# Raw weight loads from the seventh first-layer piece on are begun by ScalarE instead of SyncE

## Chip, core and metric

The kernel runs on one core of one Trainium2 chip. The metric is the device time of one execution in microseconds (us). Before the change its median over 3 runs is 1234.65 us (1234.53 to 1234.99). PE is TensorE, DVE VectorE, ACT ScalarE, POOL GpSimd, SP SyncE; SP does no arithmetic here, it begins transfers.

## What is computed

Attention over 8 batches and 12 heads (448 positions, head width 64) with RMS-normalised q and k, followed by a two-layer network with an ELU over all 3584 positions. The reference, cut to what matters:

```python
q_n, k_n = rmsnorm(q, g_q), rmsnorm(k, g_k)
scores = scale * q_n @ k_n.T
attn = exp(scores - max) / (sum + 1e-9)
x = (attn @ v).transpose(0, 2, 1, 3).reshape(B * S, H * D)   # 3584 x 768
h = x @ w_in                                                # w_in 768 x 2048
g = where(h > 0, h, exp(min(h, 0)) - 1)
out = g @ w_out                                             # w_out 2048 x 768
```

## The kernel before

The work is cut into 48 pairs of heads with 7 score tiles each, and 8 batches of the network. Every fp32 operand is split into a high and a low fp16 part, so that each product is three fp16 matmuls. The weights go through the same splitting once, at the start: `w_in` in 16 pieces of 128 x 768 (768 KB as read), `w_out` in 24 pieces of 128 x 512 (512 KB as read). For each piece `conv` builds a list of steps: `load` (a transfer from device memory into a raw buffer, L228 to L231), `s_act` on ACT (absolute value, L237, the first reader of the raw bits), `s_bits` on ACT (L240), `s_shift` on DVE (L245), `s_join` on DVE (L269, the last reader of the raw buffer), `s_sums` on PE (L142), `s_scale` on DVE, `s_high` on POOL, `s_low` on DVE (L290, L312). There are six raw buffers for `w_in` (two in `raws`, four in `whos`) and two for `w_out`, so a later load waits until the piece that had its buffer has passed `s_join`.

Order is written out by hand. The table `SCHED` gives each step a time in half slots; `run_tasks` emits the steps of a half slot, loads of whole slots first. Every engine then works through its own instructions in exactly that order. All transfers, 750 of them, are begun by SP: loads of q and k (`nat`, L330), of v (L172, L338), of the weights (L229), transposes in the transfer engines (`qkt` L420, `ptall` L613), two copies per pair that swap the halves of the transposed q (`q_swap`, L427), and the output (L711). PE needs the swapped copy for the second matmul of each score tile (L537).

The other ACT steps that matter here: `s_exp` (L558), the copy of normalised scores out of PSUM that frees the bank (`s_hi`, L592 or L598), `qk_square` (L353), `k_high` (L391), `q_high` (L401).

Of the kernel before, what the change touches and what calls it, by code (L numbers as in the profile page):

```python
# [33 lines left out]
def tile_attention_then_elu_mlp(ctx: ExitStack, tc: tile.TileContext, qk, v, v_scan, gg, w_in, w_out, out):  # L34
# [13 lines left out]
    nc = tc.nc  # L48
# [76 lines left out]
    def room(all, width, i):  # L125
        n = all.shape[1] // width
        return all[:, i % n * width : i % n * width + width]

    def small(name, w=1, dt=F32, bufs=2):
        return pool.tile([128, w], dt, tag=name, name=name, bufs=bufs)  # L130
# [3 lines left out]
    def upper(t):  # L134

        return t.bitcast(BF16).rearrange("p (n w) -> p n w", w=2)[:, :, 1]

    def column_sums(parts, bank):


        for i, a in enumerate(parts + [tiny]):
            nc.tensor.matmul(bank[:, S:], ones, a, start=i == 0, stop=i == len(parts))  # L142

    def largest(bank, e):
        nc.vector.tensor_reduce(out=e, in_=bank[:, S:], axis=AX.X, op=ALU.max)  # L145
        return e
# [3 lines left out]
    def ibits(dst, src, s1, op0, s2, op1):  # L150
        nc.vector.tensor_scalar(
            out=dst.bitcast(I32), in0=src.bitcast(I32), scalar1=s1, scalar2=s2, op0=op0, op1=op1
        )
# [53 lines left out]
    def on_pe(fn):  # L207

        late.add(fn)
        return fn  # L210
# [7 lines left out]
    def conv(src, i, width, acol, bank, parts):  # L218

        raw = raw_in[i % len(raw_in)] if width == WI_W else room(raws, 2 * width, i)
        raw, raw16 = (r.rearrange("p (n w) -> p n w", n=width) for r in (raw, raw.bitcast(U16)))

        t, w = room(wts, width, i), room(w32s, width, i if width == WI_W else i + 2)
        ws = None

        def load():  # L228
            nc.sync.dma_start(  # L229
                out=raw, in_=src[i].bitcast(U32).rearrange("p (n w) -> p n w", w=2)  # L230
            )  # L231

        def s_act():

            nc.scalar.activation(t, raw[:, :, 1].bitcast(F32), AF.Abs, scale=2.0**-112)  # L237

        def s_bits():
            nc.scalar.activation(  # L240
                raw16[:, :, 2], raw16[:, :, 1], AF.Copy, scale=0.875 * 2.0**-13, bias=0.49
            )

        def s_shift():
            nc.vector.tensor_scalar(  # L245
                out=t.bitcast(U32), in0=t.bitcast(U32), scalar1=3, scalar2=None,
                op0=ALU.logical_shift_left,
            )

        def s_sums():  # L250
            column_sums([upper(t[:, a : a + 64]) for a in range(0, width, 64)], bank)

        def s_scale():
            nonlocal ws
            e = largest(bank, acol)
            ws = small("ws", bufs=4)

            ibits(ws, e, POWER, ALU.bitwise_xor, POWER, ALU.bitwise_and)
            if width == WO_W and i % 12 == 11:
                d = i // 4 - 2  # L260
                for r in range(4):
                    rows = slice(32 * r, 32 * r + 32)
                    ibits(
                        a_out[rows, d : d + 3], most[rows, 4 * d + r : 4 * d + 12 : 4],
                        POWER, ALU.bitwise_and, 0, ALU.bitwise_or,
                    )

        def s_join():
            nc.vector.scalar_tensor_tensor(  # L269
                out=w.bitcast(U32), in0=raw[:, :, 1], scalar=0x80000007, in1=t.bitcast(U32),  # L270
                op0=ALU.bitwise_and, op1=ALU.bitwise_or,
            )

        steps = [load, s_act, s_bits, s_shift, s_join, on_pe(s_sums), s_scale]
        for fn in parts:
            step = lambda fn=fn: fn(w, ws)
            steps.append(on_pe(step) if fn in late else step)
        loads.add(load)
        return steps

# [857 lines left out]
```

## Time and profile before

| | us |
|---|---|
| median of 3 runs | 1234.65 |
| the profiled execution, its own time | 1238.01 |
| its span on the core | 1236.2 |
| PE busy in the span | 1185.0 |
| DVE busy | 863.4 |
| ACT busy | 808.2 |
| POOL busy | 499.1 |

The profiled execution is one run; 1.8 us of its time lie outside the span of the recorded instructions. A busy PE is a PE with a matmul in flight. The times of the rows below are counted from the start of the span.

### The profile page before, as it was taken

How to read it: one execution, taken by the hardware profiler on the slowest of the kernel's cores; microseconds unless marked ns; L12 is line 12 of the kernel's file. 1: busy time of each engine (PE TensorE's matmuls, PEld its weight loads, DVE VectorE, ACT ScalarE, POOL GpSimd, SP SyncE). 2: the span in 40 equal slices, each digit the busy share in tenths (PEclk: the TensorE clock that was granted, in tenths of full speed). 3: DMA queues.
4: the chain of work that ended last, by engine and by line, in shares of the span. 5: the costliest groups of instructions: out<-in, count | busy, mean ns of one | idle time of the engine just before them, and what ended most of it. 6: DMA issues, size and time to landing. Idle time of an engine off the chain costs nothing.

```text
span 1236.2 us, 21611 instructions
## 1 busy us (share of the span) xinstructions
PE 1185.0 (96%) x7180; PEld 736.4 (60%) x7180; DVE 863.4 (70%) x2042; ACT 808.2 (65%) x1705; POOL 499.1 (40%) x789
## 2 busy tenths in 40 slices
PE   3778899999999999999999999999999999999998
PEld 2556455765557655675557655675557655675576
DVE  7889999888885588666885588566785588542410
ACT  7889999867775477556675477556675477542310
POOL 4767554644444343444344343444344344320000
PEclk9889999999999999999999999999999999999999
DMA  8766889879667876687668867687568766551000
GB/s 302 224 155 189 190 185 188 164 175 193 134 137 165 177 137 135 138 195 153 128 131 162 184 139 131 137 199 150 130 131 165 181 137 134 109 108 31 1 16 30
DMA packets 403024, 181.29 MB, mean 147 GB/s; under 512 B 368352, under 2 KB 385376, under 8 KB 402912
## 3 DMA queue, kind: packets, MB, share of 16 engines
q1 hardware_dynamic: 402912, 179.91, 66.8%
q8 instruction: 57, 0.93, 0.3%
q14 instruction: 55, 0.45, 0.1%
HBM read 68.35 MB, written 11.01 MB: 64 GB/s over the span
## 4 chain that ended last, share of the span: by engine, by line
PE 82%; DVE 4%; issue 0%; ACT 0%; POOL 0%; ACTq 0%
PE m L741 23%; PE m L730 22%; PE s L741 12%; PE s L730 11%; PE s L537 9%; PE av L630 7%; DVE p L603 1%; DVE st L544 0%; DVE gall L687 0%; DVE w32s L269 0%; DVE e L674 0%; DVE wlos L312 0%; PE av L142 0%; DVE wts L245 0%; ACT s L558 0%
## 5 line engine op out<-in xcount | busy, mean ns | idle before, releaser
L544 DVE TENSOR_REDUCE st<-s 128x1 f32<-128x448 f32 x336 | 207.3, 620 | 168.4 <-PE s L537 166.8
L741 PE MATMUL m<-gall,whos 128*128 128x448 f16 x1024 | 282.0, 353 | 0.0
L562 POOL TENSOR_SCALAR st<-st 128x1 f32<-128x1 f32 x294 | 74.3, 253 | 482.2 <-ACT s L558 475.2
L741 PEld LDWEIGHTS <-whos 128*128 128x128 f16 x1536 | 221.7, 144 | 73.4 <-issue 0.7
L730 PE MATMUL m<-x,whi 128*128 128x448 f16 x926 | 256.4, 353 | 0.3 <-DVE e L674 0.3
L558 ACT ACTIVATE s<-s,st 128x448 f32<-128x448 f32 x294 | 178.1, 606 | 100.0 <-DVE st L544 98.6
L730 PEld LDWEIGHTS <-whi 128*128 128x128 f16 x1536 | 149.8, 98 | 137.2 <-issue 1.7
L598 ACT ACTIVATE p<-s,st 128x448 f16<-128x448 f32 x294 | 185.1, 631 | 61.2 <-DMA ptall<-p 35.9
L603 DVE SCALAR_TENSOR_TENSOR p<-s,st,p 128x448 f16<-128x448 f32 x294 | 198.6, 677 | 30.8 <-ACT p L598 29.6
L537 PE MATMUL s<-qkt 128*128 128x448 f16 (+1 forms) x768 | 184.8, 360 | 18.0 <-ACT gall L592 5.3
L741 PE MATMUL m<-gall,wlos 128*128 128x448 f16 x512 | 181.3, 354 | 0.0
L730 PE MATMUL m<-x,wli 128*128 128x448 f16 x463 | 163.3, 353 | 0.0
L741 PE MATMUL s<-gall,whos 128*128 128x448 f16 x512 | 140.8, 353 | 0.0
L741 PEld LDWEIGHTS <-wlos 128*128 128x128 f16 x768 | 110.6, 144 | 41.6 <-issue 6.8
L730 PE MATMUL s<-x,whi 128*128 128x448 f16 x450 | 124.0, 352 | 0.0
L730 PEld LDWEIGHTS <-wli 128*128 128x128 f16 x768 | 75.1, 98 | 74.2 <-issue 6.8
L537 PEld LDWEIGHTS <-qkt 128*128 128x128 f16 (+1 forms) x768 | 63.3, 101 | 79.4 <-issue 34.5
L684 ACT ACTIVATE gall<-e,ui 128x448 f16<-128x448 f32 x128 | 85.1, 665 | 32.1 <-DVE e L679 32.1
L630 PE MATMUL av<-ptall,vt 128*64 128x448 f16 x924 | 94.7, 353 | 0.6 <-DVE most L145 0.6
L687 DVE SCALAR_TENSOR_TENSOR gall<-e,ui,gall 128x448 f16<-128x448 f32 x128 | 88.0, 688 | 8.5 <-ACT gall L684 8.3
L382 POOL TENSOR_TENSOR nat<-nat,r 128x896 f32<-128x896 f32 (+1 forms) x48 | 84.4, 1758 | 21.8 <-DVE r L372 13.5
L741 PE MATMUL s<-gall,wlos 128*128 128x448 f16 x256 | 90.6, 354 | 0.0
(120 smaller groups left out, 1696.5 us busy)
## 6 DMA issues: line engine op xcount, KB each, us to landing
nat<-in_qk SPq DMA_DIRECT2D x48, 448.0 KB, 4.6
raws<-in_w_out SPq DMA_DIRECT2D x24, 512.0 KB, 4.1
qkt<-qkt SPq DMA_DIRECT2D x96, 112.0 KB, 4.1
out<-y SPq DMA_DIRECT2D x48, 224.0 KB, 2.4
vn<-in_v SPq DMA_DIRECT2D x38, 256.0 KB, 3.0
vscan<-in_v_scan SPq DMA_DIRECT2D x36, 224.0 KB, 3.2
whos<-in_w_in SPq DMA_DIRECT2D x10, 768.0 KB, 6.6
ptall<-p SPq DMA_TRANSPOSE x336, 3.0
```

Source lines behind the costliest of these rows:

```text
L382: nc.gpsimd.tensor_tensor(out=n[:, a:], in0=n[:, a:], in1=r[:, a:], op=ALU.mult)
L537: nc.tensor.matmul(ps[r0 : r0 + n, :S], lhs, qq[:, 1, h * S : h * S + S], start=(t == 0), stop=(t == 2),)
L544: nc.vector.tensor_reduce(out=st[:, 0:1], in_=pss[T][:, :S], axis=AX.X, op=ALU.max, negate=True)
L558: nc.scalar.activation(e, ps, AF.Exp, bias=st[:, 0:1], accum_out=st[:, 1:2])
L562: (nc.vector if by_pe(T) else nc.gpsimd).tensor_scalar(out=st[:, 1:2], in0=st[:, 1:2], scalar1=1e-9, scalar2=2.0 ** (UP - 7) if by_pe(T) e ...
L598: nc.scalar.activation(p16[:, :S], pss[T][:, :S], AF.Copy, scale=stats[T][:, 2:3])
L603: nc.vector.scalar_tensor_tensor(out=p16[:, S:], in0=ps[:, :S], scalar=r, in1=p16[:, :S], op0=ALU.mult, op1=ALU.subtract)
L630: nc.tensor.matmul(av[64 * h : 64 * h + 64, :S], vs[:, h], ps[h], start=(k == 0), stop=(k == len(terms) - 1),)
L684: nc.scalar.activation(g[:, 0], e, AF.Copy, scale=ui)
L687: nc.vector.scalar_tensor_tensor(out=g[:, 1], in0=e, scalar=ui, in1=g[:, 0], op0=ALU.mult, op1=ALU.subtract)
L730: nc.tensor.matmul(ph[:, :S], w[:, c, :], x[:, r, :], start=(c == 0 and i == 0), stop=last)
L741: nc.tensor.matmul(py[:, :S], w, g[:, r, :], start=(f == 0 and i == 0), stop=last)
```

## The change

The transfer of `load` is begun by SP for the first six pieces of `w_in`, and by ACT for the other ten and for all 24 pieces of `w_out`. Nothing else differs: same half slots, same buffers, same sizes.

```diff
         def load():
-            nc.sync.dma_start(
+            eng = nc.sync if src is w_in and i < 6 else nc.scalar
+            eng.dma_start(
                 out=raw, in_=src[i].bitcast(U32).rearrange("p (n w) -> p n w", w=2)
             )
```

The order on PE, DVE and POOL is the same in both kernels; 34 transfers leave SP's list and stand in ACT's. Code below line 228 is one line further down in the changed kernel, so L237 there is L238, L558 is L559, and so on. `whos<-in_w_in` and `raws<-in_w_in` are loads of `w_in`, `raws<-in_w_out` of `w_out`; `wts<-` is `s_act`, `raws<-raws` and `whos<-whos` are `s_bits`, `ex,st<-` is `s_exp`, `gall<-` and `ptall<-` with 112x4x128 are `s_hi`.

First place: ACT, where the load of the last `w_in` piece comes in. Before:

```order
L558 ACTIVATE ex,st<-s_69,st 128x448
L592 ACTIVATE gall<-s_67 112x4x128
L558 ACTIVATE ex,st<-s_70,st 128x448
L592 ACTIVATE gall<-s_68 112x4x128
L237 ACTIVATE wts<-whos 128x768
```

After:

```order
L559 ACTIVATE ex,st<-s_69,st 128x448
L230 DMA whos<-in_w_in 128x1536
L593 ACTIVATE gall<-s_67 112x4x128
L559 ACTIVATE ex,st<-s_70,st 128x448
L593 ACTIVATE gall<-s_68 112x4x128
L238 ACTIVATE wts<-whos 128x768
```

The load now stands three ACT instructions ahead of `s_act`, which reads what it brings.

Second place: ACT, a little later, at the second piece of `w_out`. Before:

```order
L558 ACTIVATE ex,st<-s_67,st 128x448
L240 ACTIVATE raws<-raws 128x512
L558 ACTIVATE ex,st<-s_68,st 128x448
L237 ACTIVATE wts<-raws 128x512
L558 ACTIVATE ex,st<-s_69,st 128x448
```

After:

```order
L559 ACTIVATE ex,st<-s_67,st 128x448
L241 ACTIVATE raws<-raws 128x512
L230 DMA raws<-in_w_out 128x1024
L559 ACTIVATE ex,st<-s_68,st 128x448
L238 ACTIVATE wts<-raws 128x512
L559 ACTIVATE ex,st<-s_69,st 128x448
```

Here one ACT instruction lies between the load and its reader.

Third place: SP, around the swap copies (`qkt<-qkt`) of the second pair of heads. Before:

```order
L420 DMA_TRANSPOSE qkt<-t_249 128x7x128
L229 DMA whos<-in_w_in 128x1536
L427 DMA qkt<-qkt 64x896 x2
L229 DMA raws<-in_w_in 128x1536
L420 DMA_TRANSPOSE qkt<-t_402 128x7x128 x2
L229 DMA whos<-in_w_in 128x1536
```

After:

```order
L421 DMA_TRANSPOSE qkt<-t_249 128x7x128
L428 DMA qkt<-qkt 64x896 x2
L421 DMA_TRANSPOSE qkt<-t_402 128x7x128 x2
L428 DMA qkt<-qkt 64x896 x2
L331 DMA nat<-in_qk 128x896
```

The weight load that stood directly ahead of the two swap copies is gone from SP's list, and so is the one behind them.

## Rows read from the trace of the kernel before

**Rows 1.** Busy time by stretch: start:end, length, each engine, granted clock, DMA share, GB/s.
```profile
core 0: us, PE busy (x) PEld busy (x) DVE busy (x) ACT busy (x) POOL busy (x), PEclk, DMA share, GB/s
...
100.00:150.00 50.00, 41.50 (x348) 27.29 (x347) 47.42 (x141) 48.83 (x99) 32.02 (x40) 1.00 0.66 162
150.00:200.00 50.00, 47.12 (x330) 25.82 (x329) 48.75 (x115) 48.61 (x96) 25.38 (x37) 1.00 0.94 197
...
300.00:1100.00 800.00, 800.00 (x4647) 486.05 (x4647) 565.52 (x1323) 518.28 (x1156) 321.56 (x549) 1.00 0.72 148
```

**Rows 2.** Line 229 from 22 to 245 us: loads, ns min/median/max; time to landing.
```profile
L229 SPq DMA_DIRECT2D raws<-in_w_out x24: 327/336/1157, 87.9 to 239.3; - x24
...
DMA to landing us min/median/max: 3.4/4.5/9.0
```

**Rows 3.** The page's DMA issues: count, KB of one, median us to landing.
```profile
raws<-in_w_out SPq DMA_DIRECT2D x24, 512.0 KB, 4.1
qkt<-qkt SPq DMA_DIRECT2D x96, 112.0 KB, 4.1
```

**Rows 4.** SP's queue from 27 us: start, length, line, what it begins.
```profile
31.20 0.57 SPq L229 DMA_DIRECT2D whos<-in_w_in  x1
32.28 1.11 SPq L427 DMA_DIRECT2D qkt<-qkt  x2
```

**Rows 5.** Those two swap copies: who waited for them, and their time to landing.
```profile
  PE s L537: 1.7, 1
...
DMA to landing us min/median/max: 6.7/6.7/6.8
```

**Rows 6.** PE from 36 us: start, length, line, tiles, idle time before and releaser.
```profile
39.60 0.53 PE L537 MATMUL s<-qkt 128*128 128x448 f16 x1 [1.74 <-DMA qkt<-qkt]
```

**Rows 7.** Busy time by stretch, around that wait (columns of rows 1).
```profile
38.00:42.00 4.00, 2.40 (x13) 2.21 (x14) 2.88 (x11) 1.82 (x6) 2.62 (x5) 0.57 0.63 155
42.00:46.00 4.00, 4.00 (x30) 3.26 (x30) 2.61 (x9) 3.83 (x6) 2.42 (x3) 0.57 0.00 0
```

**Rows 8.** ACT from 43 us (columns of rows 6).
```profile
43.27 0.57 ACT L401 ACTIVATE t<-nat 128x448 f16<-128x448 f32 x1
...
47.80 0.94 ACT L237 ACTIVATE wts<-raws 128x768 f32<-128x768 f32 x1
```

**Rows 9.** ACT from 99 to 111 us (columns of rows 6).
```profile
100.26 0.62 ACT L558 ACTIVATE ex<-s,st 128x448 f32<-128x448 f32 x1
...
102.44 0.91 ACT L237 ACTIVATE wts<-whos 128x768 f32<-128x768 f32 x1
...
103.86 0.60 ACT L592 ACTIVATE gall<-s 112x512 f32<-112x512 f32 x1
...
108.35 1.34 ACT L240 ACTIVATE raws<-raws 128x512 uint16<-128x512 uint16 x1
...
110.21 0.67 ACT L237 ACTIVATE wts<-raws 128x512 f32<-128x512 f32 x1
```

**Rows 10.** PE from 102 us (columns of rows 6).
```profile
105.39 0.57 PE L537 MATMUL s<-qkt 128*64 128x448 f16 x4
```

**Rows 11.** ACT from 127 and from 150 us (columns of rows 6).
```profile
127.44 0.63 ACT L558 ACTIVATE ex<-s,st 128x448 f32<-128x448 f32 x1
...
130.76 0.66 ACT L237 ACTIVATE wts<-raws 128x512 f32<-128x512 f32 x1
...
150.80 0.66 ACT L666 ACTIVATE e<-e,one 128x448 f32<-128x448 f32 x1
...
154.26 0.68 ACT L237 ACTIVATE wts<-raws 128x512 f32<-128x512 f32 x1
```

**Rows 12.** ACT's queue at line 391 (ns, first and last start); ACT then.
```profile
L391 ACTq EVENT_SEMAPHORE  x1: 38/38/38, 94.9 to 94.9; - x1
...
94.19 1.94 ACT L240 ACTIVATE whos<-whos 128x768 uint16<-128x768 uint16 x1
```

**Rows 13.** SP's waits: waiting line, releaser: us in total, times, longest.
```profile
SPq L229 <- DVE w32s L269: 26.3, 11, 5.5
```

## The prediction, made before the result was known

> **What bounds the kernel now.** I first read busy time by stretch [rows 1]. From 300 to 1100 us PE is busy for all 800 us, at a granted clock of 1.00: there the kernel is bound by matmuls, their number is unchanged, and nothing that happens on ACT or SP can show in the time unless PE is made to wait. So the change is decided in the start-up, while weights are still being split. There PE is not full: 41.50 of 50 us from 100 to 150, 47.12 from 150 to 200. The engines beside it are: ACT has 48.83 and 48.61 of 50 us, DVE 47.42 and 48.75. All 34 moved loads lie between 22 and 240 us, 29 of them before 200. In that stretch ACT and DVE together set when PE gets its tiles, and ACT has 1.17 and 1.39 us of idle time in the two stretches of 50. Whatever is put on ACT there can hardly be absorbed. What PE loses before about 205 us is lost for good, since it is full afterwards.
>
> The second thing I read is who waits for transfers. PE's matmul at 39.60 us stood 1.74 us idle for a swap copy of q [rows 6]. The two swap copies were begun at 32.28 us, right behind a 768 KB weight load begun at 31.20 on the same queue [rows 4], and took 6.7 us to land [rows 5], where the median of all 96 is 4.1 [rows 3].
>
> **The change part by part.** *Taken from SP:* 34 issues, the 24 of `w_out` with a median of 336 ns [rows 2]; at that price they are 11.4 us of SP's own time, and the waits of these loads for their buffers. SP computes nothing; the one place where I see PE pay for it is the wait above, so I count only that.
>
> *Swap copies out of the load's shadow (term A).* With the load of 31.20 us gone to ACT, where its place comes some 6 us later, the swap copies can land nearer to the median, 2.6 us sooner (6.7 - 4.1). PE gains at most its wait, 1.7 us; I take -1.7. The far end: at 38 to 46 us the granted clock is 0.57 as a mean [rows 7], that is mostly the lower of the two levels, 1.2 GHz, and the fall came while PE was idle in this very wait. If the shorter wait kept PE at 2.4 GHz, the 2.40 and 4.00 us of busy time would shrink by the factor 0.57, by 1.0 and 1.7 us. The ends of A are 0 and -4.4.
>
> Here a rule of the Trainium skill speaks against the change. The row shows a copy that waited behind a load in one queue. "DMA: Bandwidth & Descriptors", section "Issuing engines are not separate DMA queues", says that transfers run on the same 16 DMA engines whoever begins them, and that a second issuer saves only the time to issue. By that rule A is 0, since the same bytes are moved, and the sum would be 1.7 us more; the row differs only in that the load also comes later.
>
> *Two loads that come too late (terms B and C).* In SP's queue a load ran well ahead of ACT. In ACT's list it can't be begun before ACT's own sequence reaches it, and its first reader, `s_act`, stands a fixed number of ACT instructions behind. If the transfer takes longer than these, ACT itself stops, and everything behind it on ACT: exponentials (DVE and POOL wait for their sums) and the copies that free PSUM banks for PE. The transfer takes 3.4 us at the least, 4.5 at the median of these loads, 9.0 at the most [rows 2].
>
> B: the last `w_in` piece stands behind the exponential that starts at 100.26 us, its reader started at 102.44 [rows 9], a gap of 2.2 us. With 4.5 us to land, ACT stops for 2.3 us. Ends: 1.2 (3.4 us to land) and 6.8 (9.0).
>
> C: the second piece of `w_out` stands behind the `s_bits` that starts at 108.35 us, its reader started at 110.21 [rows 9], a gap of 1.9 us. With the 4.1 us of loads of `w_out` [rows 3], ACT stops for 2.2 us. Ends: 1.5 (3.4) and 7.1 (9.0).
>
> B and C add up, since ACT works from 99 to 111 us without a pause: 4.5 us. What of it reaches PE: the copy of 103.86 us ends at 104.46, and PE's score matmul that needs its bank starts at 105.39 [rows 9, 10], so 0.9 us of B are slack there. Of ACT's own idle time, 1.17 us in this stretch, I let half absorb: 4.5 - 0.6 = 3.9 us are left on ACT's chain, and I count 3.9 as the delay of the end.
>
> *Further tight pairs (term D).* Five more pairs before 200 us have gaps like these two: 3.3 us (127.44 to 130.76) and 3.5 us (150.80 to 154.26) [rows 11]. At 4.1 us to land they would stop ACT by 0.8 and 0.6, the five together by about 3.7. Against it: ACT's queue runs ahead of its arithmetic. While `s_bits` ran from 94.19 to 96.13 us, the queue had already handled, at 94.9, the wait that belongs to the second instruction behind it (L391; L353 stands between) [rows 12]. So a load may begin up to two instructions earlier than I have put it, which at some 0.6 us each closes gaps of 0.8 and 0.6. I take 1.2, a third of 3.7; the ends are 0 and 3.7. The same running ahead would shorten B and C, whose shortfalls are too large to vanish. The loads of the pieces before have gaps of 4.5 us (43.27 to 47.80) [rows 8] and more, and I count them at nothing at a landing of 4.5; if a busy queue makes it 9.0, ACT stops for up to 4.5 there, partly in idle time.
>
> *Issue on ACT (term E).* Each issue takes ACT's queue about 336 ns, 29 of them before 200 us, 9.7 us in all [rows 2]. I take 0: most stand behind an instruction of 0.6 to 1.9 us, and the queue does its work under cover of that [rows 12]. If the cover is missing, the cost is 9.7 us, in a stretch without slack.
>
> *Waits added to ACT.* A load that waits for its buffer (for `s_join` on DVE) now holds ACT's list: behind it stand the exponentials and PSUM copies for which DVE and PE wait. SP stood 26.3 us in 11 such waits, 5.5 at the longest [rows 13], but it came early; ACT comes to the same place later, when DVE has mostly passed. I take 0; the far end is one full wait, 5.5 us. Below nothing it can't go, since ACT had no such wait.
>
> Sum: -1.7 + 3.9 + 1.2 + 0 + 0 = **+3.4 us**. Against the profiled execution of 1238.01 us that is 1241.4; that run is 3.4 us above the median of 1234.65, so against the median the forecast is 1234.65 + 3.4 = **1238.0 us**.
>
> **The rivals.**
>
> *Issue isn't covered (slower still).* Then E is 9.7 us at its end; 29 issues at 336 ns on an engine that is 97% busy. For: ACT's idle time is 2.56 us in 100 us [rows 1]. Against: the queue that runs ahead [rows 12]. Time: 1238.0 + 9.7 = 1247.7.
>
> *Nothing to be seen.* The running ahead closes D and most of B and C (two instructions of 0.6 us each, 1.2 off each of 2.3 and 2.2, leaves 2.1 on ACT), and A gives 1.7 back: +0.4, 1235.0. With no ACT stop and no gain at the swap copy, only SP's 11.4 us are saved, PE waits as before, and the time is 1234.7. That last is what the rule of the Trainium skill above comes to. That the change doesn't do what it says belongs here, and the order speaks against it: the loads do stand in ACT's list.
>
> *Faster.* The mechanism is the swap copy at 39.60 us and the clock behind it. If the copy lands over 1.7 us sooner and PE's clock then does not fall, A is -4.4. Together with the 2.1 of the case above, less the 0.9 of slack at 105 us [rows 9, 10], the sum is -4.4 + 2.1 - 0.9 = -3.2: 1231.4. It decides as soon as B and C together leave less than about 2 us. For: clock and wait stand in the rows. Against: ACT and DVE are so full behind it that a gain at 46 us has to pass through ACT's list, with a load in it at 43.27 us.
>
> **How the numbers follow.** Forecast (+1 to +6.5 us, by B, C and D at their nearer ends) 0.44; issue not covered 0.12; nothing to be seen 0.25; faster 0.19. The predicted time is that of the likeliest, 1238.0 us. The measurement can tell about 0.2%, 2.5 us. Of the forecast some 0.05 lie within that, and of the faster case 0.03: faster 0.16, same 0.33, slower 0.51. The range reaches into the faster case and, by half of E, into the uncovered one: 1231.5 to 1245.5 us, with about 0.1 left out on either side.
>
> **What would show it.** In the changed kernel's trace, `s_act` of the last `w_in` piece and of the second `w_out` piece should have idle time on ACT before them, ended by the transfers, of about 2 us each; PE should wait less for the swap copy near 39 us; PE's busy time should be full from a few us later than before. If ACT's idle time stands before instructions right behind an issue, E is the cause. If ACT waits nowhere for weights, B and C are wrong; if the low clock at 38 to 45 us is gone, the faster case is under way. A changed time with the same PE idle time before 205 us would overthrow the whole reading.

## The result, and the profile after

The changed kernel takes 1248.54 us in the median of 4 runs (1245.67 to 1256.08), the kernel before 1234.78 us beside it: a ratio of 1.0114, 95% interval 1.0089 to 1.0139, 13.8 us slower. The direction was forecast; the time lies 3 us above the range and 10.5 us above the predicted 1238.0.

The profiled execution took 1249.42 us. By stretch, with the columns of [rows 1]:

```profile
50.00:100.00 50.00, 38.13 (x311) 26.61 (x310) 39.96 (x103) 42.89 (x78) 31.52 (x34) 0.90 0.77 197
100.00:150.00 50.00, 41.34 (x335) 29.60 (x335) 42.92 (x127) 44.93 (x93) 28.46 (x37) 0.93 0.56 159
150.00:200.00 50.00, 45.22 (x300) 23.81 (x297) 46.93 (x111) 46.60 (x91) 25.66 (x37) 1.00 0.87 177
200.00:250.00 50.00, 46.95 (x319) 29.10 (x319) 42.52 (x99) 43.08 (x87) 23.95 (x35) 1.00 0.78 158
...
300.00:1100.00 800.00, 800.00 (x4654) 484.02 (x4652) 569.52 (x1328) 520.80 (x1162) 327.25 (x553) 1.00 0.73 150
```

As the prediction had it, nothing happens from 300 us on. Between 100 and 200 us ACT is no longer full: 8.5 us idle where it had 2.6 [rows 1]. PE's 41.34 us from 100 to 150 hide a loss, since part of that work ran at a lower granted clock (0.93). What the prediction did not expect stands in the line of 200 to 250 us. The same line of before:

```profile
200.00:250.00 50.00, 49.67 (x338) 31.64 (x336) 45.67 (x99) 43.24 (x83) 30.25 (x41) 1.00 0.80 170
```

PE was nearly full there, and now loses another 2.7 us.

The loads themselves, from 22 to 245 us, and what waited for them [rows 2]; then the page's DMA issues [rows 3]:

```profile
L230 ACTq DMA_DIRECT2D raws<-in_w_out x23: 334/335/637, 87.1 to 236.5; - x23
...
  ACT wts L238: 10.3, 7
...
DMA to landing us min/median/max: 3.4/4.5/9.8
raws<-in_w_out ACTq DMA_DIRECT2D x24, 512.0 KB, 4.0
```

An issue costs what it cost SP (335 ns against 336), and the median landing has not moved. But now `s_act` on ACT waits for loads, which was 1.0 us in before. The readers that wait, on ACT (start, length, line, tiles, idle time before and what ended it; the first is the last piece of `w_in`, the others pieces 1, 6, 10, 13, 18 and 22 of `w_out`, counted from 0):

```profile
105.89 0.91 ACT L238 ACTIVATE wts<-whos 128x768 f32<-128x768 f32 x1 [1.81 <-DMA whos<-in_w_in]
114.91 0.66 ACT L238 ACTIVATE wts<-raws 128x512 f32<-128x512 f32 x1 [1.46 <-DMA raws<-in_w_out]
136.36 0.68 ACT L238 ACTIVATE wts<-raws 128x512 f32<-128x512 f32 x1 [0.94 <-DMA raws<-in_w_out]
160.67 0.68 ACT L238 ACTIVATE wts<-raws 128x512 f32<-128x512 f32 x1 [0.20 <-DMA raws<-in_w_out]
177.15 0.68 ACT L238 ACTIVATE wts<-raws 128x512 f32<-128x512 f32 x1 [0.83 <-DMA raws<-in_w_out]
...
210.20 0.70 ACT L238 ACTIVATE wts<-raws 128x512 f32<-128x512 f32 x1 [2.05 <-DMA raws<-in_w_out]
...
241.91 0.68 ACT L238 ACTIVATE wts<-raws 128x512 f32<-128x512 f32 x1 [3.06 <-DMA raws<-in_w_out]
```

The first four have partners in [rows 9, 11]: they started at 102.44, 110.21, 130.76 and 154.26. So the delay against before grows from 3.5 to 4.7, 5.6 and 6.4 us, by 1.2, 0.9 and 0.8 us. The first two steps are about the idle time of the reader (1.46 and 0.94), the third is more than it (0.20). But 3.5 us are there already at the first, of which its own wait is only 1.8. The rest comes from an earlier place, on PE. In the kernel before PE had two waits near 75 us, after:

```profile
74.35 0.35 PE L537 MATMUL s<-qkt 128*128 128x448 f16 x1 [1.34 <-DMA qkt<-t]
76.82 1.28 PE L537 MATMUL s<-qkt 128*128 128x448 f16 x3 [2.12 <-DMA qkt<-qkt]
```

The same two in the changed kernel:

```profile
77.31 0.53 PE L538 MATMUL s<-qkt 128*128 128x448 f16 x1 [5.06 <-DMA qkt<-t]
78.33 1.28 PE L538 MATMUL s<-qkt 128*128 128x448 f16 x3 [0.49 <-DMA qkt<-qkt]
```

There PE waited 5.06 us for a transpose of the normalised q and k (`qkt<-t`), not for the swap copies. It leaves this place 1.5 us later than before (78.33 against 76.82). SP's queue, ACT's queue, and the time to landing of these two transposes:

```profile
64.38 3.55 SPq L421 DMA_TRANSPOSE qkt<-t  x2
64.80 0.36 ACTq L230 DMA_DIRECT2D raws<-in_w_in  x1
DMA to landing us min/median/max: 10.6/10.8/10.9
```

Ahead of all this lies what the change gains, the place of [rows 6, 7]:

```profile
38.80 0.54 PE L538 MATMUL s<-qkt 128*128 128x448 f16 x2 [1.43 <-ACT ptall L593]
42.00:46.00 4.00, 3.46 (x36) 2.62 (x36) 3.79 (x13) 4.00 (x9) 2.48 (x3) 1.00 0.86 261
```

The wait for the swap copy is gone (a wait of 1.43 us for ACT stands close to its place), and here the granted clock from 42 to 46 us is 1.00, not 0.57.

So the profile gives three candidates: loads that land after their reader is due ("late"), transposes that are slow beside loads of another queue ("beside"), and the issues on ACT ("issue", the rival of the prediction).

### The profile page after: what moved, and what is told of

Read it like the earlier page. It is cut to its first block, busy times and chain, and to the rows that moved or that the text cites. A ratio compares the mean times of both kernels' runs of the same rounds, so it can differ in the third digit from the quotient of the medians.

```text
span 1247.6 us, 21596 instructions
## 1 busy us (share of the span) xinstructions
PE 1190.4 (95%) x7180; PEld 739.8 (59%) x7180; DVE 864.5 (69%) x2042; ACT 808.2 (65%) x1705; POOL 496.5 (40%) x789
## 4 chain that ended last, share of the span: by engine, by line
PE 77%; DVE 2%; ACT 1%; issue 0%; DMA 0%; POOL 0%; SPq 0%; ACTq 0%; POOLq 0%
PE m L742 21%; PE m L731 21%; PE s L742 11%; PE s L731 10%; PE s L538 8%; PE av L631 6%; DVE wlos L313 0%; DVE p L604 0%; ACT p L599 0%; DVE st L545 0%; DMA ptall<-p 0%; DVE w32s L270 0%; ACT s L559 0%; DVE a_out L151 0%; DVE ss L358 0%
## 5 line engine op out<-in xcount | busy, mean ns | idle before, releaser
L559 ACT ACTIVATE s<-s,st 128x448 f32<-128x448 f32 x294 | 178.2, 606 | 99.5 <-DVE st L545 98.3
L383 POOL TENSOR_TENSOR nat<-nat,r 128x896 f32<-128x896 f32 (+1 forms) x48 | 84.5, 1760 | 21.3 <-DVE r L373 12.9
```

The costliest lines, as they stand in the source:

```text
L383: nc.gpsimd.tensor_tensor(out=n[:, a:], in0=n[:, a:], in1=r[:, a:], op=ALU.mult)
L559: nc.scalar.activation(e, ps, AF.Exp, bias=st[:, 0:1], accum_out=st[:, 1:2])
```

## The experiments

All ratios are against the kernel before on the same chip, with a 95% interval; its medians there were 1235.4 to 1235.9 us, so 0.001 is 1.2 us. Gains and losses in us are worked out from the ratio, which is not the quotient of the two medians: for e6 and e7 the medians lie 9.1 and 4.6 us apart, where the ratios give 7.8 and 3.7. Pieces are counted from 0.

**e1: 34 issues on ACT and nothing else.** The kernel before, with an additional transfer of 8 bytes per partition, begun by ACT, at each place of a moved load. Nobody reads what they bring.

```diff
+            if src is w_out or i >= 6:
+                k = 10 + i if src is w_out else i - 6
+                nc.scalar.dma_start(out=tinies[:, 2 * k : 2 * k + 2], in_=src[i].bitcast(U32)[:, :2])
```

> The kernel before, in which SP still begins all 34 weight loads; at the same places ACT begins 34 further transfers of 8 bytes per partition into a tile that nobody reads. So ACT pays for 34 issues and for nothing else. Theory 'late' (ACT stands still because the data of a late load isn't there) and theory 'beside' (a load on a second queue and a transpose on SP's queue slow each other) expect the time of the kernel before, within 1 us. Theory 'issue' (each issue stops ACT) expects 34 issues of 0.34 us, of which 29 lie where ACT is full: 5 to 10 us above before.

1235.22 us, ratio 0.9996 (0.9986 to 1.0007). Issuing on ACT costs nothing that can be measured; the rival "issue isn't covered" falls.

**e2 and e3: take one suspect out.** A list of the pieces whose load ACT begins takes the place of the change's condition, here and in most of what follows. e2 puts the seven loads that were waited for back on SP, e3 those beside slow transposes.

```diff
-            nc.sync.dma_start(
+            on_act = [6, 7, 8, 9, 10, 11, 12, 13, 14] if src is w_in else [0, 2, 3, 4, 5, 7, 8, 9, 11, 12, 14, 15, 16, 17, 19, 20, 21, 23]
+            (nc.scalar if i in on_act else nc.sync).dma_start(
```

> The changed kernel, with the seven loads for which ACT visibly stood still (w_in piece 15; w_out pieces 1, 6, 10, 13, 18, 22) given back to SP; 27 loads stay with ACT. The idle times of ACT before their first readers add up to about 10 us in the changed kernel's trace. 'Late' expects most of that back: 1248.5 - 7 to 10, that is 1239 to 1242 us. 'Beside' expects the loss between 55 and 78 us (about 4 us) to stay and the later ones to shrink only a little: 1245 to 1248. 'Issue' expects 7 of 34 parts of the loss back: about 1246.

1237.04 us, ratio 1.0026 (1.0005 to 1.0046).

```diff
+            on_act = [7, 8, 9, 10, 11, 13, 15] if src is w_in else [0, 1, 2, 3, 4, 5, 6, 7, 8, 9, 10, 11, 12, 13, 15, 16, 18, 19, 20, 21, 22, 23]
```

> The changed kernel, with five other loads given back to SP: those that took 7 us or more to land, or were in flight while SP's transposes took 7 us or more (w_in pieces 6, 12, 14; w_out pieces 14, 17). ACT does not stand still for any of them. 'Beside' expects the loss between 55 and 78 us (4 us) and that around 200 us (about 2 us) back: 1241 to 1244 us, and no transpose above 7 us there. 'Late' expects nothing back from it: 1247 to 1250. 'Issue' expects 5 of 34 parts back: about 1246.5.

1246.74 us, ratio 1.0087 (1.0068 to 1.0105). Most of the loss hangs on the seven late loads. What e3 gives back is less than its profile shows early on: its transposes near 64 us land after 3.3 and 4.6 us, and PE's matmul behind the swap copies starts 5.1 us earlier than in the changed kernel (73.22 against 78.33). But then ACT waits longer for pieces 1, 13 and 22 than in the changed kernel, and the reader of piece 22 starts only 3.1 us earlier:

```profile
73.22 0.91 PE L538 MATMUL s<-qkt 128*128 128x448 f16 x3 [1.72 <-DMA qkt<-qkt]
...
111.55 0.66 ACT L238 ACTIVATE wts<-raws 128x512 f32<-128x512 f32 x1 [2.34 <-DMA raws<-in_w_out]
...
174.36 0.67 ACT L238 ACTIVATE wts<-raws 128x512 f32<-128x512 f32 x1 [2.32 <-DMA raws<-in_w_out]
...
238.83 0.68 ACT L238 ACTIVATE wts<-raws 128x512 f32<-128x512 f32 x1 [3.73 <-DMA raws<-in_w_out]
```

So the losses by slow transposes and by late loads do not simply add. Back to e2: three of e2's ten runs lay at 1243.7 to 1244.2, the other seven at 1235.0 to 1237.8; more on that below.

**e4: the loads earlier in ACT's list.** If they are late, let them start sooner: each load up to 6 half slots earlier, as far as its buffer is free in the written order.

```diff
-        [56.5, 58.5, 60, 60, 62.5, 63, 67, 68.5, 70],
+        [50.5, 58.5, 60, 60, 62.5, 63, 67, 68.5, 70],
...
-        [51.5, 68.5, 70, 70.5, 71, 73, 77, 77, 78.5],
+        [47.0, 68.5, 70, 70.5, 71, 73, 77, 77, 78.5],
```

> The changed kernel, ACT begins the same 34 loads, but each up to 6 half slots earlier in ACT's list, as far as the raw buffer is free in the written order (w_in 15 and w_out 1 by 6 half slots; w_out 13, 18 and 22 by 0.5 to 1 only). 'Late' expects the idle times before the readers of w_in 15 and w_out 1 (3.4 us together) and part of those of w_out 6 and 10 to go: 1243 to 1246 us. 'Beside' expects no gain of that kind, since as many loads lie beside transposes: 1246 to 1252. 'Issue' expects no change: 1248.

1252.16 us, ratio 1.0135 (1.0116 to 1.0154): slower still. ACT's waits in it, from 20 to 245 us (us in total, times, longest):

```profile
ACT s L559 <- DVE w32s L270: 2.6, 2, 1.3
...
ACT wts L238 <- DVE w32s L270: 2.3, 1, 2.3
...
ACT wts L238 <- DMA raws<-in_w_out: 1.4, 2, 1.0
```

The waits for landings of weight loads have nearly gone, as "late" wanted. In their place ACT's instructions stand behind loads that wait for a buffer: L270 is `s_join` on DVE, the last reader of the raw buffer, which no exponential needs. ACT's waits for `s_join` come to 7.0 us in all, of a loss of 16.7; the rest was not divided further. In ACT's in-order list a load was too late for its reader or too early for its buffer. SP's list stood 26.3 us in such waits [rows 13], with no arithmetic behind them.

**e6 and e7: one suspect alone.** The seven late loads on ACT and all others on SP; then only the two of terms B and C.

```diff
+            on_act = [15] if src is w_in else [1, 6, 10, 13, 18, 22]
```

> The complement of e2: only the seven loads whose reader was seen to wait (the last w_in piece, w_out pieces 1, 6, 10, 13, 18, 22) are begun by ACT, all others by SP. 'Late' (a load in ACT's list lands after its reader is due, and ACT stops): these seven carry most of the loss, 1243 to 1246 against some 1235.4 for the kernel before, with ACT's s_act idle for transfers by 1 to 3 us each. 'Beside' (loads on a second queue hold up the transposes of t): with seven loads, none of them beside the transposes of 64 us, 1235 to 1238. 'Additive no' (a third reading: what is lost in one place is absorbed or made up by the others): between, 1238 to 1243.

1244.74 us, ratio 1.0063 (1.0044 to 1.0083): 7.8 us.

```diff
+            on_act = [15] if src is w_in else [1]
```

> Only the last w_in piece and the second w_out piece are begun by ACT: the prediction's terms B and C alone. The prediction's working gives +3.9 us for them, 1238 to 1241 with its ends wider. 'Late' by the trace of the changed kernel (idle time of 1.81 and 1.55 before the two s_act): +3.0 to +3.5, 1238 to 1239. 'Absorbed' (ACT's or PE's slack behind them takes it up): within 1 us of the kernel before, 1235 to 1236.5.

1240.24 us, ratio 1.0030 (1.0017 to 1.0043): 3.7 us. The two readers in e7:

```profile
102.90 0.92 ACT L238 ACTIVATE wts<-whos 128x768 f32<-128x768 f32 x1 [1.85 <-DMA whos<-in_w_in]
111.83 0.66 ACT L238 ACTIVATE wts<-raws 128x512 f32<-128x512 f32 x1 [1.37 <-DMA raws<-in_w_out]
```

3.2 us of idle time on ACT, 3.7 at the end: what ACT waits between 100 and 112 us is not absorbed. "Late" is shown as the largest part, by taking it out (e2) and by doing it alone (e6).

**e5, e9 and e10: the gain.** Five early loads on ACT; the one load of 31.20 us alone on ACT; and that load left on SP, but behind the two swap copies. In e10 nothing is on a second queue.

```diff
+            on_act = [7, 8, 9, 10, 13] if src is w_in else []
```

> Only w_in pieces 7, 8, 9, 10 and 13 are begun by ACT, loads that nobody was seen to wait for, and among them the one that the prediction's term A moves out of the swap copies' way (31.20 us). 'Late': nothing is lost, and if the 1.7 us of term A is real, 1233 to 1235; if it isn't, 1235 to 1236. 'Beside': any load on a second queue costs the transposes beside it something, 1236 to 1238.

1235.09 us, ratio 0.9987 (0.9975 to 0.9998).

```diff
+            on_act = [8] if src is w_in else []
```

> One load alone moves to ACT: w_in piece 8 (counted from 0), begun at 31.20 us before, directly ahead of the two swap copies. The prediction's term A alone: -1.7 us, with ends 0 and -4.4, so 1231 to 1235.5, most likely some 1233.9 against 1235.6 for the kernel before. If the swap copy's wait was nobody's loss: 1235 to 1236.

1234.92 us, ratio 0.9990 (0.9981 to 1.0000).

```diff
-        [11, 24, 27.5, 26.5, 28.5, 32, 31.5, 31.5, 38],
+        [11.5, 24, 27.5, 26.5, 28.5, 32, 31.5, 31.5, 38],
```

> The same load stays on SP, but stands behind the two swap copies instead of ahead of them (its half slot is 11.5 instead of 11). Nothing is on a second queue. 'The load merely stood ahead' (what the rule of the Trainium skill comes to: who begins a transfer does not matter, only when): the same gain as with the load on ACT, 1.7 us, some 1233.9, and PE no longer waits for the swap copy near 39 us. 'It must be on another queue' : no gain, 1235 to 1236, the swap copies land after over 6 us still.

1234.45 us, ratio 0.9987 (0.9976 to 0.9997). Its waits on PE for transfers, from 30 to 85 us:

```profile
51.50 0.36 PE L537 MATMUL s<-qkt 128*128 128x448 f16 x1 [0.50 <-DMA qkt<-qkt]
70.78 0.35 PE L537 MATMUL s<-qkt 128*128 128x448 f16 x1 [0.71 <-DMA qkt<-t]
72.95 0.73 PE L537 MATMUL s<-qkt 128*128 128x448 f16 x3 [1.82 <-DMA qkt<-qkt]
```

The wait of 1.74 us near 40 us [rows 6] is gone, and all three gain 1.2 to 1.6 us, whoever begins the load; each gain is little more than its interval, and that of e9 reaches 1.0000. What matters is that the load no longer stands ahead of the swap copies. That agrees with the Trainium skill, "DMA: Bandwidth & Descriptors", section "Issuing engines are not separate DMA queues", which says that transfers run on the same 16 DMA engines whichever engine begins them: the gain was 1.2 us with the load on ACT and 1.6 with it on SP.

**e8: the loads on POOL.** All 34 begun by another engine that computes, with a list that is half empty.

```diff
+            on_act = range(6, 16) if src is w_in else range(24)
+            (nc.gpsimd if i in on_act else nc.sync).dma_start(
```

> All 34 moved loads are begun by POOL, not by ACT, at the same half slots. 'Late' says that the loss comes from the load standing in an in-order list of an engine that computes, close ahead of its reader: POOL's list is only half full, so it comes to the load earlier or later than ACT did; where POOL waits for DVE (s_high waits for s_scale) it comes later. Expected: a loss again, 1239 to 1248, with ACT's s_act idle for transfers; ACT itself is never held by a load that waits for s_join. 'Second queue' (two queues at once are slow, whoever's they are): the transposes begun near 64 us again take about 10 us, and the delay at 80 us is again +2 or more over that at 55. 'ACT only' (the instruction costs on ACT): 1234 to 1237.

1267.77 us, ratio 1.0254 (1.0231 to 1.0277), beyond every expectation. An issue takes POOL 601 ns of its own time in the median, where ACT's queue took 335; ACT waits for landings again, and the transposes near 70 us are slow too. POOL's issues, ACT's waits from 20 to 275 us, and the landing of the transposes from 60 to 80 us:

```profile
L230 POOL DMA_DIRECT2D raws<-in_w_out x24: 527/601/640, 96.0 to 271.7; - x24
...
ACT wts L238 <- DMA raws<-in_w_out: 14.4, 9, 3.9
...
DMA to landing us min/median/max: 11.7/12.4/13.0
```

How the 31 us divide among these wasn't separated. "Late" and slow transposes are both not ACT's alone.

**e11 and e12: is "beside" the rest?** The two loads that ran beside the slow transposes alone on ACT; then everything on ACT but the late ones and those beside slow transposes.

```diff
+            on_act = [12, 14] if src is w_in else []
```

> Only w_in pieces 12 and 14 move to ACT, the two whose transfers ran beside the two transposes of t begun at 64 and 66 us that took 10.6 and 10.9 us to land. 'Beside': these two loads on a second queue cause it by themselves, transposes near 65 us take 7 us or more, PE loses 2 to 4 us at 65 to 80: 1237.5 to 1239.5. 'Early loss is something else' (the state of the clock, an earlier place of the transposes by the other moved loads): 1235 to 1236.5.

1234.39 us, ratio 0.9986 (0.9976 to 0.9997): no loss at all, a gain. "Beside" as written falls. The profile of e11 says where the gain is:

```profile
39.66 0.35 PE L538 MATMUL s<-qkt 128*128 128x448 f16 x1 [1.97 <-DMA qkt<-qkt]
...
72.47 0.73 PE L538 MATMUL s<-qkt 128*128 128x448 f16 x3 [0.83 <-DMA qkt<-qkt]
```

The wait near 40 us is still there, that of 2.12 us at 76.82 (2.12 in e1 too, with the order of before) has become 0.83: the mechanism of term A at a second place, where the load of piece 12 stood on SP (67.39 us) ahead of the second transpose and two swap copies.

```diff
+            on_act = [7, 8, 9, 10, 11, 13] if src is w_in else [0, 2, 3, 4, 5, 7, 8, 9, 11, 12, 15, 16, 19, 20, 21, 23]
```

> On ACT stay w_in pieces 7 to 11 and 13 and the 16 w_out pieces whose reader was not seen to wait and that were not beside slow transposes; the seven late ones, w_in 6, 12 and 14 and w_out 14 and 17 are on SP. If the two causes 'late' and 'beside' are all that the change costs, 1233.5 to 1236, and with the gain at the swap copy nearer to the lower end. If loads in ACT's list cost something by themselves (their waits for buffers, or new late ones), 1236.5 to 1240.

1237.03 us, ratio 1.0007 (0.9997 to 1.0017). With the gain near 40 us in it, some 2 us are lost elsewhere. One wait in it, from 100 to 245 us, is not in before, and the changed kernel has it too with 1.1 us: a load on ACT that waits for `s_join` and holds up `qk_square`.

```profile
ACT qkt L354 <- DVE w32s L270: 1.4, 1, 1.4
```

**e13 to e17: a loss that comes in some executions.** e2 and the changed kernel are one program up to 85 us, yet the transposes of 64 us took 6.3 and 4.7 us in e2's profile and 10.6 and 10.9 in the other. So I looked whether e2's upper runs are executions with this pile-up, in which loads of ACT's queue and transposes of SP's are under way together and all of them are slow. e13: all early loads on ACT, none of the late ones or of `w_out`. e14: e2 with piece 12 on SP. e15 and e16: e2 and the changed kernel once more.

```diff
+            on_act = range(6, 15) if src is w_in else []
```

> ACT begins w_in pieces 6 to 14, nothing of w_out and not the last w_in piece. 'Pile-up' (in some executions the transposes of 64 us and the loads of pieces 11, 14 and 12 from ACT's queue are under way together, and all of them take some 10 us): runs in two groups, one at 1233 to 1237 and some, about one in three, at 1241 to 1245. 'It is w_out' (the upper group of e2 comes from later loads): one group, 1233 to 1238.

1234.14 us (1232.61 to 1237.21, 11 runs), ratio 0.9986 (0.9975 to 0.9997): one group, where "pile-up" expected two.

```diff
+            on_act = [6, 7, 8, 9, 10, 11, 13, 14] if src is w_in else [0, 2, 3, 4, 5, 7, 8, 9, 11, 12, 14, 15, 16, 17, 19, 20, 21, 23]
```

> e2 with w_in piece 12 on SP too, in whose list it stands between the two transposes. 'Pile-up': without the third load beside the transposes there is one group, 1234 to 1239. 'Other cause': again some runs at 1243 to 1245.

1237.52 us (1234.63 to 1239.86, 12 runs), ratio 1.0011 (0.9999 to 1.0023).

> e2 once more, for its spread. 'Pile-up': again two groups, 1235 to 1238 and some runs at 1243 to 1245; where the profiled execution is of the upper group, the transposes at 64 us take some 10 us in it, where it is of the lower one, about 3 to 5. 'Chance of that one series': a single group.

1238.61 us, ratio 1.0024 (1.0004 to 1.0044); 4 of 12 runs at 1241.1 to 1245.5. Its profiled execution, at 1241.09, is one of them. ACT's load, the two transposes and their landing, of e15, and then of e2's profile (1236.77 us):

```profile
64.40 0.35 ACTq L230 DMA_DIRECT2D raws<-in_w_in  x1
64.04 3.34 SPq L421 DMA_TRANSPOSE qkt<-t  x2
DMA to landing us min/median/max: 8.8/9.3/9.8
```

```profile
63.81 0.33 ACTq L230 DMA_DIRECT2D raws<-in_w_in  x1
64.34 3.93 SPq L421 DMA_TRANSPOSE qkt<-t  x2
DMA to landing us min/median/max: 4.7/5.5/6.3
```

PE's waits behind these transposes and the swap copies, in e15 and then in e2:

```profile
74.84 0.35 PE L538 MATMUL s<-qkt 128*128 128x448 f16 x1 [2.98 <-DMA qkt<-t]
77.22 1.28 PE L538 MATMUL s<-qkt 128*128 128x448 f16 x3 [2.03 <-DMA qkt<-qkt]
```

```profile
73.94 0.73 PE L538 MATMUL s<-qkt 128*128 128x448 f16 x3 [1.50 <-DMA qkt<-qkt]
```

That is 5.0 us against 1.5, so the pile-up is 3.5 of the 4.3 us between these two executions. The time of a run alone does not show one: the runs above 1239 us of e2, e15 and e17 also have the lower mean granted clock (0.993 to 0.995, the others 0.996 to 1.000), and the kernel before has runs of 0.993 and 0.994 as high as 1240.1.

> The changed kernel once more. 'Pile-up': the runs spread over 7 us or more, 1243 to 1252, in groups, and the profiled execution shows the transposes at 64 us either at about 10 us (then it is some 4 us or more longer) or at 3 to 5. 'Always there': the transposes take 10 us again, and the times lie within 4 us.

1248.69 us (1243.31 to 1253.13), ratio 1.0102 (1.0074 to 1.0130). In its profile the transposes of 64 us land after 12.9 and 11.8 us, and there is a second pile-up: a transpose begun at 199.5 us takes 14.0 us, and the loads of `w_out` pieces 17 and 18, begun 0.3 and 0.6 us behind it, 12.3 and 13.2. In the first profile of the changed kernel the same three took 9.0, 8.6 and 9.5, and ACT waited 2.05 us (the reader at 210.20).

In all slow cases (three at 64 us, two at 200) a load of ACT's was begun 0.2 to 0.5 us behind a transpose of SP; in e2, e11 and e13 the load came 0.5 to 0.9 us ahead of it, and the transposes took 3.3 to 6.3. e17 puts this to the test: e2 with piece 12 a little earlier in ACT's list.

```diff
-        [34.5, 39, 40, 41.5, 42, 45.5, 44, 48, 49.5],
+        [33, 39, 40, 41.5, 42, 45.5, 44, 48, 49.5],
```

> e2 with the load of w_in piece 12 two instructions earlier in ACT's list (half slot 33 instead of 34.5), so that it should be begun ahead of the transposition of 64 us. 'Order decides': the upper group of e2 and e15 (8 of 22 runs at 1240 or more) is gone, 1234 to 1239, and in the profile the load is begun ahead of the transposition, which lands in 3 to 5 us. 'Order doesn't matter': about a third of the runs at 1240 or more again. If the load can't pass its wait in ACT's queue and is begun at the same time as before, nothing changes and the question stays open.

1236.28 us (1234.45 to 1242.74), ratio 1.0017 (1.0003 to 1.0031). In its profile, of a run at 1234.45, the load was begun at 63.20, 0.9 us ahead, and the transposes took 4.9 and 2.9. But 3 of its 12 runs still lie at 1240.6 to 1242.7, against 7 of 22 for e2 and e15 together (the expectation said 8). The edit doesn't remove the upper group, so that the order within half a microsecond decides is not shown. Nor does a load close behind suffice: near 40 us ten transposes had one begun 0.4 to 0.7 us behind them and took 5.3 to 7.3 us. What is shown: the slow transposes come in some executions of one program and not in others, and kernels without piece 12 on ACT (e12, e14), 24 runs, have no run at 1240 or above; nor has e13, which has it there, though e13 as a whole lies lower, and a run with a pile-up might stay below 1240.

**e18: the gain twice, without ACT.** The kernel before with two loads moved in SP's own list: piece 8 behind the swap copies near 32 us, piece 12 ahead of both transposes near 66 us.

```diff
-        [11, 24, 27.5, 26.5, 28.5, 32, 31.5, 31.5, 38],
+        [11.5, 24, 27.5, 26.5, 28.5, 32, 31.5, 31.5, 38],
...
-        [34.5, 39, 40, 41.5, 42, 45.5, 44, 48, 49.5],
+        [32, 39, 40, 41.5, 42, 45.5, 44, 48, 49.5],
```

> The kernel before with two loads moved in SP's list: w_in piece 8 behind the swap copies of 32 us (half slot 11.5), as in e10, and w_in piece 12 ahead of both transpositions of 66 us instead of between them (half slot 32). Nothing on ACT. 'Same mechanism twice': the gain of e10, 1.6 us, and up to that of e11, 1.7 us: 1232 to 1234 against 1235.8, PE's waits for swap copies at 39 and 77 us both small. 'One place is enough' (the second gain is taken up by other waits): 1234 to 1235.

1232.59 us (1231.63 to 1233.41), ratio 0.9975 (0.9965 to 0.9984): 3.1 us faster than before, and the fastest version here. PE's waits for transfers, from 30 to 85 us:

```profile
52.15 0.36 PE L537 MATMUL s<-qkt 128*128 128x448 f16 x1 [0.80 <-DMA qkt<-qkt]
72.30 0.97 PE L537 MATMUL s<-qkt 128*128 128x448 f16 x3 [0.31 <-DMA qkt<-qkt]
```

## Why the prediction was right or wrong

**What bounds the kernel.** Right that the start-up decides, and that a delay of ACT there is a delay of the end. Wrong in one sentence: "What PE loses before about 205 us is lost for good, since it is full afterwards" was used to leave out the five loads behind 200 us. PE was full there because nothing made it wait. The changed kernel has its two longest waits for loads there, 2.05 and 3.06 us (before had 1.04 at the second), and PE loses 2.7 us from 200 to 250. This is the first step that failed.

**Term A, -1.7.** Right in size: -1.2 to -1.6 us (e9, e10). That the row showed 1.74 was in part luck: with the load in its old place the same wait was 0.99 us in e1, 1.53 in e6, 1.97 in e11 and 3.15 in e7. It was counted at one place only; the same row pattern, a load ahead of swap copies and PE idle behind it, stood at 76.82 us with 2.12 us, and is worth about as much again (e11, e18). The changed kernel does not get the second gain when the transposes ahead of the copies are slow. The rule of the Trainium skill was weighed wrongly: that transfers share their engines whoever begins them does not make A zero, since what counts is the order within SP's list. The far end of A, by the clock, does not hang on the load's place: from 42 to 46 us the granted clock is 1.00 in this profile, and with the load in its old place it is 1.00 in e1, e6 and e11 and 0.54 in e7. The 0.57 that the prediction read was that of one execution.

**Terms B and C, 3.9 together.** Right: idle times of 1.81 and 1.46 us against 2.3 and 2.2 forecast, 3.7 us at the end for the two alone (e7, 2.1 to 5.3). ACT's slack was thought to absorb 0.6; nothing of that is seen.

**Term D, 1.2.** Mis-sized as put down. The pairs before 200 us cost 0.94, 0.20 and 0.83 us of ACT, 2.0 in all; with the two behind 200 us the five further loads make e6 minus e7, 4.1 us of the time (a difference of two ratios, each good to about 2 us). That ACT's queue runs ahead was the right idea: two of the five pairs before 200 us made no reader wait.

**Term E, 0.** Right (e1).

**Waits for buffers, 0.** Too low: one load that waits for `s_join` holds ACT by 1.1 us in the changed kernel and 1.4 in e12. The argument was that ACT comes later than SP, when DVE has mostly passed. That holds for all but one place, and e4 shows what happens when it doesn't.

**What was not in the sum.** The landing times were taken as those of before, 4.5 us at the median, 9.0 at the most. The median stayed; the transposes were never looked at, and they are where a second queue hurt: 10.6 and 10.9 us at 64 us, 9.0 to 14.0 at 200. By PE's two waits near 75 us, 3.46 in before and 5.55 after, and by the 2.05 us at 210.20, this is some 4 us in the profiled execution. This is the second step that failed: a term that the sum did not have, and for which no reason was given. How much of it reaches the end is less sure: e3, without the slow transposes at 64 us, is 1.9 to 3.3 us below the changed kernel by the ratios (1.0087 against 1.0102 and 1.0114), with intervals that overlap. The granted clock fell behind the first late loads as well (0.76 from 115 to 120 us, 0.66 from 140 to 145, both 1.00 in before); what that cost was not separated.

Put together from runs: seven late loads +7.8 (e6), everything else +3.2 (e2, its upper runs included), 11.0 against a whole of 14.1 by the ratio (11.0 to 17.2). The pile-up at 200 us, in which pieces 17 and 18 were both on ACT, is in neither and fits what is left; it was not measured alone, and e3 shows that such parts need not add. What makes a pile-up come or not in a given execution stays open.

## What to carry to other kernels

A queue that only begins transfers holds up no arithmetic while it waits for a buffer (SP stood 26.3 us in such waits here); an engine that computes does, and a load in its list is bound between the last reader of its buffer and the first reader of its data. Measure the distance from the load's place to its reader in that engine's own instructions, for every load of the list to its end, against the landing time. Before moving transfers to another issuer, look whether a changed order in the old list does the same: here two moved rows gave 3.1 us.

## What the runs showed of the hardware that was not expected

Transfers of two queues can slow each other. Stretches around the slow transposes, of the changed kernel, and of e2, where they were not slow (columns of [rows 1]):

```profile
66.00:74.00 8.00, 6.25 (x51) 3.35 (x47) 7.28 (x20) 8.00 (x14) 5.15 (x7) 1.00 1.17 128
64.00:72.00 8.00, 6.70 (x58) 3.75 (x54) 6.30 (x20) 8.00 (x14) 6.48 (x8) 1.00 0.96 240
```

The DMA engines are reported as fully busy in both (1.17 and 0.96) and move 128 GB/s in one and 240 in the other. Where no weight load is on a second queue (before, e10, e18), no transpose of q and k up to 250 us took more than 5.7 us. With loads on ACT it is not general: over the other profiles but those of e1 and e8, 18 transposes had a load of ACT's begun 0.1 to 0.7 us behind them, and they took 4.9 to 14.0 us, 12 of them under 7.5. What decides is not known.

ACT's queue begins a load further ahead of its place than the two instructions that [rows 12] showed: in e2 the load of piece 12 began at 63.81 us, while the four instructions ahead of it in ACT's list started only at 64.13, 64.61, 65.08 and 65.69.
